# Attention and feed-forward on one core: batch 0's queries and group 0's tokens in two halves, in a newly ordered program

## The chip, the cores and the metric

The kernel runs on one core of a Trainium2 chip. The time is the device time of one execution in microseconds (us); the median of the runs counts. A profile is one more execution, recorded by the hardware profiler.

The engines are named as in the profile: PE is the matmul engine (PEld its weight loads), ACT applies functions such as exp and relu, DVE does elementwise work, POOL is used here for small copies and to issue software DMA, and SP issues hardware DMA. Each engine works through its own instructions in the order in which the program gives them.

## What is computed

```python
scores = scale * q @ k.T                    # 8 batches, 8 heads, 576 positions, 64 wide
bias   = bias_table[bucket(|i - j|)]        # constant from distance 128 on
attn   = softmax(scores + bias)
x      = (attn @ v)  as (4608 tokens, 512)
y      = relu(x @ w_in) ** 2 @ w_out        # 512 -> 2048 -> 512
```

Inputs and weights come in fp16 tiles after loading; the output is fp32. 4608 tokens are 8 batches of 576.

## The kernel before, in words

**An order made by a planner.** The kernel does not emit instructions as its loops run. Every step (one operation on one engine, with its inputs, its buffers, an estimated length and a due time) is handed to `P.add`. `P.schedule` then walks simulated engine clocks and picks, for each engine, the step that can start first; among those, the one with the smallest due time. It fixes each engine's order and which slot of a buffer ring a step uses. On the chip there is no choice left: an engine that reaches an instruction whose input is not there stands still, with everything behind it. Due times come from formulas (`nominal(p)`, `G0 + GP * g`) and are overridden by a long table, `DUES`, of step numbers and times.

**Attention.** Heads are taken in pairs; pair p belongs to batch p // 4. q and k of batches 0 and 1 are loaded as 96 rows of six positions, turned by PE (L718, twelve 96x96 transposes into an f bank), and copied to `qt` and `kt` by ACT (L680) or DVE (L682). The last 64 of the 576 positions need block-diagonal copies `qz` (L745, on DVE or POOL). Later batches are turned by SP's DMA (L701). Scores have keys on partitions: for a key tile of 128, two heads at once in two row tiles, two matmuls 512 wide (L763) into one of two set banks `st`; ACT takes exp of 1024 columns into `pt` (L776). Last queries (L789, exp L799) and last keys (L814, exp L824) have steps of their own and use set banks too. DVE multiplies by the exponential of the bias near the diagonal (L857): per pair four pieces of 512, 1536, 640 and 192 columns. Where the bias is constant, nothing is multiplied. Then PE makes the values: for each query tile nine matmuls (L893, L900), three query tiles in one step and two in another; DVE divides (L917, L922) into `x`. `pt` has three slots.

**Turning x.** For batches 0 and 1, `x_turn` turns x on PE (L960, four 128x128 for a query tile) and ACT or DVE copies it to `xt` (L680, L682).

**Feed-forward.** Tokens are in nine groups of 512. Layer 1 of a group has 16 steps, one per 128 hidden columns: four matmuls 512 wide (L1315) into one of three f banks, relu on ACT (L1344), square on DVE (L1354) into `g`. It needs all of the group's `xt` and the quarter of `w_in` that holds the columns. Layer 2 (L1084) works with sums of weights (L1014) and of activations (L1039); groups 7 and 8 do part of layer 1 with seven products in place of eight (L1239), which are fed in among the rest.

**Loads.** `loader` (L327) issues them. POOL's software queue has eight lanes and carries q, k and v of batches 0 and 1, the four quarters of `w_in`, four of `w_out` (512 KB each), and the rows of later q and k. SP and ACT issue the first q and k, the tables, and later v. In POOL's order these issues stand among its qz copies.

Of the kernel before, what the change touches and what calls it, by code (L numbers as in the profile page):

```python
# [43 lines left out]
UNITS = {7: 1, 8: 2}  # L44

# [19 lines left out]
0:118000 10:143030 32:114040 40:-9780 51:205280 56:-2470 58:-21460 60:-36430 62:-2100 64:-42740 66:-3570  # L65
70:-12220 72:-22540 74:-4430 76:-1710 80:-25480 84:-30350 88:-3160 90:-27100 94:-10280 98:-12060 102:-10140
120:5110 122:3790 124:10370 126:15880 128:17190 130:347580 132:-52240 134:-14320 136:-8260 138:-11000 140:-8690
142:-36670 144:-30540 146:-36280 148:-3170 150:-2780 152:-2780 154:-2290 156:-2220 158:-2580 160:-2620 168:-1450
170:-29000 172:-2120 174:5970 176:2720 200:17220 204:10300 206:2310 210:2020 220:10760 222:10420 226:9730
228:17470 238:412520 244:14860 256:9990 266:59150 282:8490 304:235630 312:-44250 326:288120 340:211140  # L70
383:449450 436:233270 560:-10510 562:7970 570:63210 586:-18300 588:3090 590:7540 594:8390 614:9280 618:9490
620:9600 622:9600 624:9600 644:9910 648:10090 650:8530 657:130160 660:15000 674:27510 676:78210 703:84310
730:389740 735:120980 743:21470 745:-6240 747:10350 760:424020 771:160200 774:117470 802:255000 813:21690
824:65160 892:84330 896:150530 906:116620 907:140670 914:201640 961:53470 979:52250 998:16050 1008:-16370
1051:35570 1076:6550 1096:-26430 1120:214110 1179:37190 1211:39430 1216:389710 1221:131080 1222:203470
1229:68730 1255:140120 1256:112580 1257:187030 1313:200990 1343:211010 1344:216260 1347:299680 1354:193070
1373:113930 1376:86680 1378:116480 1392:2880 1405:123690 1410:124790 1437:128150 1442:124910 1444:3730
1469:126520 1474:123310 1497:272360 1506:47770 1531:134590 1533:159790 1546:203540 1560:530 1564:117960
1586:145220 1587:144260 1618:167550 1626:54840 1676:5070 1685:70350 1690:162240 1706:278460 1709:19830
1710:292470 1742:312270 1744:290020 1759:206510 1766:233170 1780:224870 1804:197130 1807:-22280 1839:-14530  # L80
1850:3140 1895:196650 1907:22680 1923:302060 1931:294800 1935:98210 1952:321510 1957:298250 1960:319370
1979:377200 2031:5800 2044:235210 2047:324240 2052:207380 2058:222320 2116:53050 2198:-1850 2220:2260
2223:212770 2293:433240
# [159 lines left out]
def kernel(  # L243
# [78 lines left out]
    def loader(eng_name, eng, out_, in_, packets, deps=(), bufs=(), due=0.0, after=0.0, turn=-1e9):  # L322

        lane = [Buf(r_lane)] if eng_name == "POOL" else []
        issue = P.add(
            {eng_name: (775.0 if packets[0] >= 512 else 665.0) if eng_name == "POOL" else 500.0},
            lambda: io(eng.dma_start(out=out_(), in_=in_())),  # L327
            deps,
            list(bufs) + lane,
            due,  # L330
            after,
        )
        return P.land(packets, [issue], list(bufs) + lane, spare[0]), issue
# [6 lines left out]
    def const(f):  # L340
        return lambda: f

    def load(*args, **kw):
# [8 lines left out]
            const(t[0, 0:2].rearrange("h (p j) d -> p h (j d)", j=6)), (192, (60, 60)[w]), (), [b_stg[0]], due=-5,  # L352
# [7 lines left out]
        (128, 27), due=0,  # L360
# [136 lines left out]
    def load_six(p, w):  # L497
# [8 lines left out]
                (192, 61), (), [b_stg[p]], pdue(),  # L506
# [3 lines left out]
    def load_rows(p, w):  # L510
# [8 lines left out]
                (512, 13.2), s_fix, [b_stg[p]], pdue(),  # L519
            )  # L520
            for e in range(2)
# [5 lines left out]
                (128, 13.2), s_fix, [b_stg[p]], pdue(),  # L527
# [14 lines left out]
    def load_v_head(b, h):  # L542
        l = load(
            "POOL", nc.gpsimd,
            lambda: vas[b_v[b].slot][:, :, h, 0:64],
            const(v[b, h, 0:512, :].rearrange("(t p) d -> p t d", p=128)),
            (512, 13.2), v_fix[min(b, 1)], [b_v[b]], pdue(),
        )
        l_v.setdefault((b, h // 2), []).append(l)

    def load_v_tail(b):
        for e in range(2):
# [4 lines left out]
                (256, 13.2), v_fix[min(b, 1)], [b_v[b]], pdue(),  # L557
# [4 lines left out]
    def load_v(b):  # L562
        for tt in range(4):
# [4 lines left out]
                (1024, 13.2), v_fix[min(b, 1)], [b_v[b]], pdue(),  # L568
# [7 lines left out]
    def load_v_fp32(b):  # L576
# [9 lines left out]
        for tt in range(5):  # L586
            fb = Buf(r_f)
            if tt < 4:
# [5 lines left out]
                        (1024, 18.0), 690.0,  # L594
                    )
                ]
            else:
# [5 lines left out]
                        (256, 18.0), 450.0,  # L603
# [67 lines left out]
    xt_ready, x_last = {}, {}  # L671
# [17 lines left out]

    def pair(p):  # L690
# [5 lines left out]
        for w, dst in ((0, qts), (1, kts)):  # L696
            if b >= DT_QK:
# [9 lines left out]
                evac.append(P.land((640, 23.0), [o], [qb, b_stg[p]], SPARE[1]))  # L707
# [31 lines left out]
        for w, src, dst in ((0, qts, qzs), (1, kts, kzs)):  # L739
            for e in range(2):  # L740
# [6 lines left out]
                spread.append(one_of({"DVE": 205.0, "POOL": 320.0} if b < DT_QK else {"POOL": 320.0}, sp, [evac[w]] + z_fix[min(p, 1)], [qb], T - 1000))  # L747
        pb = Buf(r_pt)
        exps = {}

        def p5(t):
            return t[:, 0:PW].rearrange("p (j e s) -> p j e s", j=4, e=2)
# [91 lines left out]
        def view(o0, dims):  # L844
            t = pts[pb.slot]
            full = t[:, o0 : o0 + 1]
            return bass.AP(tensor=full.tensor, offset=full.offset, ap=[full.ap[0]] + [list(d) for d in dims])

        def tab(w0, n, rep):
            full = tb_sb[:, 2 * hp : 2 * hp + 2, w0 : w0 + n]  # L850
            return bass.AP(
                tensor=full.tensor, offset=full.offset,
                ap=[full.ap[0]] + ([[0, rep]] if rep > 1 else []) + [list(x) for x in full.ap[1:]],
            )

        def tt(a, t):
            io(nc.vector.tensor_tensor(out=a, in0=a, in1=t, op=MULT))  # L857

# [3 lines left out]
                lambda: tt(view(0, [[S, 2], [1, 256]]), tab(128, 256, 1)),  # L862
# [4 lines left out]
                lambda: tt(view(2 * S, [[2 * S + 128, 2], [S, 2], [1, 384]]), tab(0, 384, 2)),  # L867
# [4 lines left out]
                lambda: tt(view(6 * S + 256, [[S, 2], [1, 320]]), tab(0, 320, 1)),  # L872
# [8 lines left out]
        xb = x_bufs[p] = Buf(r_x)  # L881
        norms = []
        for part, qt0, nq in ((0, 0, 3), (1, 3, 2)):
            bank = Buf(r_pv)

            def pv(qt0=qt0, nq=nq, bank=bank):
                ps = pv_ps[bank.slot][:, 0 : nq * 130].rearrange("p (t e d) -> p t e d", t=nq, e=2)
                pt, pm = pts[pb.slot], p4s[pb.slot]
                va, vm = vas[b_v[b].slot], v4s[b_v[b].slot]
                for i in range(nq):  # L890
                    c = (qt0 + i) * 128
                    io(
                        nc.tensor.matmul(  # L893
                            ps[:, i, :, :], pm[:, c : c + 128], vm[:, hp, :, 0:65], start=True, stop=False
                        )
                    )
                    for e in range(2):
                        for jt in range(4):
                            io(
                                nc.tensor.matmul(  # L900
                                    ps[:, i, e, :],
                                    pt[:, (2 * jt + e) * S + c : (2 * jt + e) * S + c + 128],
                                    va[:, jt, 2 * hp + e, 0:65],
                                    start=False,
                                    stop=(jt == 3 and e == 1),
                                )
                            )

            o = P.add(
                {"PE": nq * 300.0}, pv,  # L910
                bands + list(exps.values()) + l_v[b, hp] + first, [bank, pb, b_v[b]], T + 1, after, "f",
            )
            rb = Buf(r_r)

            def recip(nq=nq, bank=bank, rb=rb):
                ps = pv_ps[bank.slot][:, 0 : nq * 130].rearrange("p (t e d) -> p t e d", t=nq, e=2)
                io(nc.vector.reciprocal(out=rs[rb.slot][:, 0:nq], in_=ps[:, :, :, 64:65]))  # L917

            def norm(nq=nq, bank=bank, rb=rb, qt0=qt0):
                ps = pv_ps[bank.slot][:, 0 : nq * 130].rearrange("p (t e d) -> p t e d", t=nq, e=2)  # L920
                io(
                    nc.vector.tensor_tensor(  # L922
                        out=xs[xb.slot][:, qt0 : qt0 + nq, :].rearrange("p t (e d) -> p t e d", e=2),
                        in0=ps[:, :, :, 0:64],
                        in1=rs[rb.slot][:, 0:nq].to_broadcast([128, nq, 2, 64]),
                        op=MULT,
                    )
                )

            o = P.add({"DVE": 190.0}, recip, [o], [bank, rb], T - 2000)  # L930
            o = P.add({"DVE": dve(nq * 128)}, norm, [o], [bank, rb, xb], T - 2000)
            norms.append(o)
# [488 lines left out]
```

## Time and profile before

| | us |
|---|---|
| runs, median (lowest to highest) | 372.38 (371.84 to 373.97) |
| the profiled execution | 371.38 |
| span of its profile | 369.6 |
| PE busy | 355.2 (96%) |
| DVE busy | 274.9 (74%) |
| ACT busy | 261.8 (71%) |
| POOL busy | 183.6 (50%) |
| first exp of attention (L776) | 9.66 |
| first layer-1 matmul (L1315) | 41.35 |
| first relu (L1344) | 42.42 |

The span runs from the first to the last recorded instruction; what lies around it is 1.8 us. "Busy" counts modelled ends, so that a PE full of back-to-back matmuls reads as 100%. In the profile's lines, `out<-in` gives the program's names of tiles, `xN` a count, and the bracket the engine's idle time before the piece and what ended it. In the page's slices a digit is the busy share of a slice of 9.24 us, in tenths.

### The profile page before, as it was taken

The page shows a single profiled execution, that of the slowest core. Times are in us where ns is not written, and L with a number is a line of the kernel's source. Part 1 is how long each engine was busy: PE and PEld are TensorE (multiplying, and loading weights), DVE is VectorE, ACT ScalarE, POOL GpSimd, SP SyncE. Part 2 cuts the span into 40 slices and gives each one's busy share as a digit, 9 for nine tenths or more (in the row PEclk, how much of TensorE's full clock was granted, in tenths as well). Part 3 has the DMA queues.
Part 4 walks back from the last instruction along what each step waited for, and adds up shares of the span by engine and source line. Part 5 has one row for each costly group of instructions (what it writes and reads, how often), then busy time and mean ns, then how long its engine had stood idle before and what let it go on. Part 6 is the DMA issues. An engine that isn't in the chain of part 4 may idle for free.

```text
span 369.6 us, 10056 instructions
## 1 busy us (share of the span) xinstructions
PE 355.2 (96%) x3966; PEld 247.2 (67%) x3966; DVE 274.9 (74%) x626; ACT 261.8 (71%) x380; POOL 183.6 (50%) x332
## 2 busy tenths in 40 slices
PE   3887999999999999999999999999999999999996
PEld 3564655756768565877766765466777877767785
DVE  4998799958884588756695666886888569586773
ACT  4998899786686789797788777977677335546600
POOL 8986249999999898777786671011000000000000
PEclk9999899999999999999999999999999999999999
DMA  9999999999999999999999994134122130020032
GB/s 160 158 167 189 197 146 150 176 156 118 191 182 164 167 170 167 130 169 161 149 178 107 158 139 105 35 66 94 48 66 53 20 106 2 28 87 28 3 114 87
DMA packets 162293, 44.26 MB, mean 120 GB/s; under 512 B 145734, under 2 KB 162246, under 8 KB 162246
## 3 DMA queue, kind: packets, MB, share of 16 engines
q0 software_dynamic: 74208, 14.53, 51.1%
q1 hardware_dynamic: 87696, 28.80, 41.4%
q8 instruction: 31, 0.51, 0.6%
q10 hardware_dynamic: 342, 0.30, 0.3%
q14 instruction: 16, 0.13, 0.1%
HBM read 36.88 MB, written 9.44 MB: 125 GB/s over the span
## 4 chain that ended last, share of the span: by engine, by line
PE 80%; DMA 7%; POOL 5%; DVE 5%; issue 1%; ACT 1%; SPq 0%; POOLq 0%
PE f L1315 28%; PE f L1084 27%; PE pv L900 8%; PE st L763 7%; DMA ks<-in_k_dram 3%; PE pv L893 2%; DMA w_in_sb<-in_moe_w_in_dram 2%; PE st L814 2%; POOL ks L327 2%; PE st L789 1%; PE st L1239 1%; DVE pt L857 1%; DMA vm<-in_v_dram 1%; POOL qs L327 1%; POOL va L327 1%; DVE s L1039 1%
## 5 line engine op out<-in xcount | busy, mean ns | idle before, releaser
L776 ACT ACTIVATE pt<-st 128x1024 f16<-128x1024 f32 x128 | 124.4, 1026 | 23.1 <-PE st L763 22.8
L1315 PE MATMUL f<-xt,w_in_sb 128*128 128x512 f16 (+4 forms) x656 | 130.8, 338 | 0.1
L1344 ACT ACTIVATE rt<-f 128x512 f16<-128x512 f32 x132 | 77.9, 606 | 39.2 <-PE f L1315 35.7
L1315 PEld LDWEIGHTS <-w_in_sb 128*128 128x128 f16 x656 | 57.6, 98 | 45.8 <-issue 9.8
L1354 DVE TENSOR_TENSOR g<-rt 128x512 f16<-128x512 f16 x132 | 57.2, 440 | 33.1 <-ACT rt L1344 32.3
L857 DVE TENSOR_TENSOR pt<-pt,tb_sb 128x512 f16<-128x512 f16 (+2 forms) x96 | 60.4, 639 | 10.7 <-ACT pt L776 10.1
L1084 PEld LDWEIGHTS <-g 128*128 128x128 f16 x576 | 54.7, 98 | 12.5 <-issue 4.2
L327 POOL DMA_DIRECT2D ks<-in_k_dram x79 | 55.8, 725 | 9.4 <-DMA w_in_sb<-in_moe_w_in_dram 2.7
L327 POOL DMA_DIRECT2D qs<-in_q_dram x79 | 55.6, 714 | 6.5 <-DMA w_out_sb<-in_moe_w_out_dram 2.9
L900 PE MATMUL pv<-va,pt 128*128 128x65 f16 x1280 | 55.8, 194 | 0.2 <-DVE pt L857 0.2
L900 PEld LDWEIGHTS <-pt 128*128 128x128 f16 x1280 | 51.1, 98 | 3.9 <-issue 0.9
L1084 PEld LDWEIGHTS <-s 128*128 128x128 f16 x432 | 40.9, 98 | 9.2 <-issue 3.4
L1112 DVE SCALAR_TENSOR_TENSOR y<-f,y 128x512 f32<-128x512 f32 (+1 forms) x47 | 31.3, 666 | 14.9 <-PE f L1084 14.5
L763 PE MATMUL st<-qt,kt 64*128 64x512 f16 x256 | 40.7, 389 | 1.5 <-ACT pt L776 0.9
L893 PE MATMUL pv<-vm,pm 128*128 128x130 f16 x160 | 35.6, 222 | 0.8 <-DVE x L922 0.7
L1084 PE MATMUL f<-wt,g 128*128 128x256 f16 x288 | 36.2, 273 | 0.0
L1084 PE MATMUL f<-w_out_sb,s 128*128 128x256 f16 x288 | 36.1, 273 | 0.0
L1084 PE MATMUL f<-w_out_sb,g 128*128 128x256 f16 x272 | 33.8, 273 | 0.1
L745 POOL COPY qz<-qt 64x64 f16<-64x64 f16 x50 | 17.2, 345 | 33.2 <-DMA qt<-qs 23.6
L922 DVE TENSOR_TENSOR x<-pv,r 128x384 f16<-128x384 f32 (+1 forms) x64 | 31.2, 487 | 1.4 <-DVE r L917 0.2
L1039 DVE TENSOR_TENSOR s<-g,s 128x1024 f16<-128x1024 f16 x36 | 26.2, 734 | 0.1
L917 DVE RECIPROCAL r<-pv 128x6 f32<-128x6 f32 (+1 forms) x64 | 11.8, 184 | 15.2 <-PE pv L900 15.0
(92 smaller groups left out, 348.9 us busy)
## 6 DMA issues: line engine op xcount, KB each, us to landing
out_dram<-y SPq DMA_DIRECT2D x34, 256.0 KB, 2.4
f<-in_v_dram SPq DMA_DIRECT2D x24, 256.0 KB, 4.1
qs<-in_q_dram POOLq DMA_DIRECT2D x48, 64.0 KB, 4.5
ks<-in_k_dram POOLq DMA_DIRECT2D x48, 64.0 KB, 4.5
w_in_sb<-in_moe_w_in_dram POOLq DMA_DIRECT2D x4, 512.0 KB, 9.7
w_out_sb<-in_moe_w_out_dram POOLq DMA_DIRECT2D x4, 512.0 KB, 15.3
ks<-in_k_dram POOLq DMA_DIRECT2D x7, 144.0 KB, 5.5
qs<-in_q_dram POOLq DMA_DIRECT2D x7, 144.0 KB, 5.4
```

The costliest lines, as they stand in the source:

```text
L327: lambda: io(eng.dma_start(out=out_(), in_=in_())),
L763: nc.tensor.matmul(sets_ps[st.slot][:, e, :], kt[rw, ts(jt, 128)], qt[rw, 0:512], start=True, stop=True,)
L776: nc.scalar.activation(out=p5(pts[pb.slot])[:, jt, :, 0:512], in_=sets_ps[st.slot], func=EXPF, scale=SCALE)
L857: io(nc.vector.tensor_tensor(out=a, in0=a, in1=t, op=MULT))
L893: nc.tensor.matmul(ps[:, i, :, :], pm[:, c : c + 128], vm[:, hp, :, 0:65], start=True, stop=False)
L900: nc.tensor.matmul(ps[:, i, e, :], pt[:, (2 * jt + e) * S + c : (2 * jt + e) * S + c + 128], va[:, jt, 2 * hp + e, 0:65], start=False, sto ...
L922: nc.vector.tensor_tensor(out=xs[xb.slot][:, qt0 : qt0 + nq, :].rearrange("p t (e d) -> p t e d", e=2), in0=ps[:, :, :, 0:64], in1=rs[rb.s ...
L1084: nc.tensor.matmul(home[bf.slot][:, ts(s_, HALF)], left(c, s_), right(c), start=(c == 0 and (s_ == 0 or apart) and (own or i not in before ...
L1112: nc.vector.scalar_tensor_tensor(out=dst, in0=ps, scalar=OSC, in1=ys[y[plus].slot][:, cs], op0=MULT, op1=mybir.AluOpType.add,)
L1315: nc.tensor.matmul(g_ps[bank.slot][:, a:z], w_in_sb[:, kk, ts(nt, 128)], xt_sb[:, kk, c : c + z - a], start=(kk == 0), stop=(kk == 3),)
L1344: io(nc.scalar.activation(out=rts[rb.slot], in_=g_ps[bank.slot], func=RELUF))
L1354: nc.vector.tensor_tensor(out=gs[gb1.slot][:, nt, :], in0=rts[rb.slot], in1=rts[rb.slot], op=MULT)
```

## The change

Batch 0's pairs are handled in two halves of their queries: half 0 takes queries 0 to 255 (two query tiles), half 1 the other 320. The first halves of all four pairs come first (`HSTEP` sets their due times), then the second halves. Two key tiles of a half share one set bank, so an exp still has 1024 columns; last keys split into 256 and 320 columns; last keys and last queries of batch 0 move from the set banks to the f banks. The bias is multiplied in three pieces in half 0 and four in half 1. Values come as two query tiles, then three. `x_turn` of batch 0 turns its first two tiles after the first halves.

Layer 1 of group 0 (`by_halves`) takes 256 tokens at a time: eight steps for each half, and a step makes two hidden tiles of 128 columns in one f bank with eight matmuls 256 wide. Its relu has 512 columns as before; the square writes two strips of 256. The first half needs only the first 256 tokens of `xt` (`xt_half[0]`).

`DUES` is replaced as a whole, and some estimated lengths of loads change, which only the planner reads. With both, the order of the whole program is new. On POOL, qz copies number 111 in place of 101; on DVE, 17 in place of 27. Three copies of the bias table move from DVE to ACT. The other kinds of work keep their number of instructions but for a few.

```diff
+HALVES, HSTEP, HL1 = 1, 1650.0, (20000.0, 34000.0)
 DUES = """
-0:118000 10:143030 32:114040 40:-9780 ...
+8:-10082 18:14645 30:300187 31:89669 ...
 """
...
+    def half_of_pair(p, part, turned):
+        hp = p % 4
+        qb, evac, spread = turned
+        T = LEAD + HSTEP * (4 * part + hp)
+        q0 = 256 * part
+        nk = 256 if part == 0 else 320
+        def scores(jt):
+            st = Buf(r_set)
+            def score():
+                for j in range(2):
+                    for e in range(2):
+                        rw = ds(64 * e, 64)
+                        io(nc.tensor.matmul(
+                            sets_ps[st.slot][:, e, ts(j, 256)], kt[rw, ts(jt + j, 128)], qt[rw, ds(q0, 256)],
+                            start=True, stop=True,
+                        ))
...
+            exps[jt] = P.add({"ACT": act(1024)}, ex, [o], [st, pb], T)
+        def last_keys():
+            st = Buf(r_g)
...
+        scores(0)
+        last_keys()
+        scores(2)
+        if part:
+            last_queries()
...
+        return values(p, part, 2 * part, 2 + part, pb, bands + list(exps.values()), T, 0.0)
...
-            deps = [n_[0 if qt < 3 else 1] for n_ in norms]
+            deps = [n_[0 if qt < (2 if b < HALVES else 3) else 1] for n_ in norms]
...
+                if b < HALVES:
+                    xt_half.setdefault(qt // 2, []).append(e)
...
+    def by_halves(g):
+        gb1 = g_bufs[g]
+        for h in range(2):
+            for u in range(8):
+                bank, rb = Buf(r_g), Buf(r_rt)
+                due = HL1[h] + 1000.0 * u
+                def f1(u=u, h=h, bank=bank):
+                    for j in range(2):
+                        for kk in range(4):
+                            io(nc.tensor.matmul(
+                                g_ps[bank.slot][:, ts(j, HALF)], w_in_sb[:, kk, ts(2 * u + j, 128)],
+                                xt_sb[:, kk, ts(h, HALF)], start=(kk == 0), stop=(kk == 3),
+                            ))
+                o = P.add({"PE": 8 * mm(HALF)}, f1, xt_half[h] + [l_win[u // 2]], [bank, gb1], due, 0.0, "f")
...
+            if g < HALVES:
+                by_halves(g)
+            for nt in [] if g < HALVES else [nt for nt in range(16) if nt % 8 >= 2 * units]:
...
         norms = [pair(4 * b + hp) for hp in range(4)]
+        if b < HALVES:
+            norms = list(zip(*([half_of_pair(4 * b + hp, part, norms[hp]) for hp in range(4)] for part in range(2))))
```

## The prediction

> **What bounds the kernel now.** I read the page's 40 slices first, then windows of five microseconds over the start, the timeline of the two thinnest windows, PE's waits, and the groups by form for durations.
>
> ```profile
> PE   3887999999999999999999999999999999999996
> DVE  4998799958884588756695666886888569586773
> ACT  4998899786686789797788777977677335546600
> ```
>
> PE is full from the fifth slice (about 37 us) to the last but one. Only the start and the tail hold idle PE time; whatever shortens the rest must take work out of PE, and this change takes none. Windows (columns: window, length, busy time of PE, PEld, DVE, ACT, POOL, PE clock, DMA share, GB/s):
>
> ```profile
> 5.00:10.00 5.00, 4.36 (x67) 3.14 (x68) 2.98 (x11) 3.50 (x7) 4.86 (x7) 1.00 1.82 172
> 15.00:20.00 5.00, 3.71 (x74) 2.20 (x74) 4.85 (x14) 4.88 (x8) 4.51 (x7) 1.00 1.46 172
> 20.00:25.00 5.00, 4.04 (x90) 2.90 (x84) 4.79 (x13) 4.84 (x6) 3.95 (x6) 1.00 1.65 177
> 25.00:30.00 5.00, 4.25 (x83) 3.04 (x81) 4.84 (x14) 4.89 (x8) 4.67 (x9) 1.00 1.42 159
> 30.00:35.00 5.00, 3.30 (x57) 2.29 (x53) 3.99 (x13) 4.28 (x7) 2.58 (x13) 1.00 1.22 188
> 35.00:40.00 5.00, 4.59 (x60) 3.62 (x61) 3.78 (x12) 3.24 (x5) 2.87 (x5) 0.66 1.23 198
> 40.00:45.00 5.00, 5.00 (x47) 2.46 (x44) 4.10 (x13) 4.68 (x8) 1.09 (x3) 1.00 1.22 199
> 32.60:36.00 3.40, 2.02 (x40) 1.44 (x40) 2.51 (x8) 1.95 (x5) 2.48 (x13) 1.00 1.25 204
> 36.00:39.40 3.40, 3.40 (x40) 2.65 (x37) 2.26 (x7) 2.54 (x4) 1.27 (x4) 0.50 1.23 198
> ```
>
> From 15 to 30 us ACT and DVE are full (4.8 to 4.9 of 5) and PE waits on them: all it has is attention of batch 0. From 30 to 40 nobody is full: ACT falls to 3.24. Then PE runs at half clock for 3.4 us. At 41.35 layer 1 starts and PE is full. The timeline shows why 30 to 40 is thin (start, duration, engine and line, idle before with releaser):
>
> ```profile
> 35.41 0.45 PE L718 MATMUL f<-id_sb,ks 96*64 96x96 f16 x12 [1.27 <-DMA ks<-in_k_dram]
> 35.90 0.65 ACT L680 ACTIVATE kt<-f 128x576 f16<-128x576 f16 x1 [1.45 <-PE f L718]
> 39.35 1.23 ACT L824 ACTIVATE pm<-st 128x576 f16<-128x576 f32 x2 [0.72 <-PE st L814]
> 41.35 1.03 PE L1315 MATMUL f<-xt,w_in_sb 128*128 128x512 f16 x4
> ```
>
> PE stands before a transpose of keys whose DMA has not landed, and ACT stands behind PE. The chain of waits names the transfer: issued at 26.07, it took 9.29.
>
> ```profile
> 26.07 9.29 DMA ks<-in_k_dram
> ```
>
> A busy PE overstates, since ends are modelled. So I counted slots from start to start: 216 ns for a 512-wide matmul, 109 for a 256-wide, 29 for a 65-wide one. PE's work is 332.4 us, and 145 switches between row-tiled scores and whole-array matmuls take 0.1 each, 14.5. The rest of the span is loss: 5.5 before the first matmul; in five-microsecond steps from 5 us on 2.5, 0.5, 1.45, 1.5, 1.2, 2.5 and 1.9; later 2.7 in all; 3.1 after the last matmul. Up to 40 us that is 5.5 + 11.55 = **17.05 us**, the only store a change of order can draw on.
>
> **The change part by part.** *Layer 1 of group 0 in halves.* 64 matmuls of 216 ns become 128 of 109: 13.95 - 13.82 = +0.13 us on PE. The 109 is a slot between 256-wide matmuls whose weights also change each time:
>
> ```profile
> L1084 PE MATMUL f<-wt,g 128*128 128x256 f16 x288 | 36.2, 273 | 0.0
> ```
>
> and from the chain, with start and length:
>
> ```profile
> 81.68 1.73 PE f L1315 x8
> 164.84 1.75 PE f L1084 x16
> ```
>
> (1.73/8 = 216 ns, 1.75/16 = 109). Here a rule speaks against the change: the Trainium skill, TensorE: Matmul & The Clock Gate, Back-to-back issue gap, gives for a stream of weight load and matmul about 81 ns at width 128 and 131 at 512. Interpolated, 256 wide would take some 98, and halving would cost 128 x 98 - 64 x 131 = +4.1 us, turning the forecast into a loss. The trace has 216 and 109, so I keep +0.13. Weight loads double (64 more of 98 ns) but fit under 109. The relu stays 128x512 (606 ns). The square writes two strips of 256: nearest row 440 ns (128x512), at most the 500 of a 640 band; x16 that is 0 to +1 us on DVE, behind PE's matmuls once layer 1 runs.
>
> *Batch 0 in halves.* On PE the scores keep their columns: 32 of 512 become 64 of 256, +0.05. Program order has 151 switches in place of 145: +0.6. **PE work: about +0.8 us in all**, paid for certain. On ACT the last keys' exp splits 576 into 256 and 320. By the rows of 512 (604), 576 (657) and 1024 (1026) an exp takes about 172 ns + 0.832 per column, so 385 + 438 against 651: +0.17 x 4 = +0.7; three table copies (0.6 each) move from DVE to ACT, +1.8. On DVE the bands of a pair go from 465 + 952 + 500 + 258 to seven pieces, by the same rows +0.5 x 4; the table copies (0.69 x 3) and ten qz copies (about 0.25) leave: DVE is not longer. POOL gets those ten copies, 0.33 each, **ahead of loads in its queue** (rival C). Splits below a row's size carry +-0.1 each; over the 20 pieces I take 0, keep -0.5 to +1.
>
> *What is moved.* Layer 1 can start when two token tiles of batch 0 are turned. ACT's order up to the first relu, at saturated spacing (0.915 for 1024, 0.545 for 576, 0.49 for 512): before 18 x 0.915 + 13 x 0.545 + 9 x 0.49 = 28.0; it started at 9.66 and came to its first relu at 42.42, so it waited 4.8. After: 16 x 0.915 + 9.8 for the rest = 24.4, none of it exps of pair 4. At the start q is cast first and the copies to q and k of pair 0 follow directly; from the cast and copy rows the first exp comes at about 8.5, 1.1 earlier. ACT then gets to the relu at about 33 if it never waits.
>
> *PE's ledger after.* First matmul: 5.5 as before. 5 to 10: 2.5 becomes 1.4 (first exp earlier). 10 to 30: ACT-bound in both, 4.65 kept. By then PE has done 18.8 us of work and switches, and 18.8 + 11.55 gives the first layer-1 matmul at about 30.3, where before it came at 41.35 after 24.7 of work. From 30 to 42 PE has 256-wide layer-1 groups to stand between pairs. What I find late next: the second group needs w_in's second quarter (about 35.1), keys of pair 5 (about 32.9), and POOL's copies for pair 5 (about 0.9 us of waiting). A walk by hand gives 0.9 to 1.3 there in place of 4.4; a walk has no jitter, and the queues of before showed 9.29 us for one small load, so I add 0.7 to 1.2: **2.0**. Sum: 5.5 + 1.4 + 4.65 + 2.0 = 13.5.
>
> *The clock.* Of the 4.4 lost, 1.7 is the half clock from 36.0 to 39.4. The trace shows it after a window in which PE was busy 2.02 of 3.40, with no gap over 1.27. The same page of the Trainium skill, HAM oscillation, warns of PE-idle gaps over about 3.4 us; by that, nothing here should slow it. By the rule the after has no dip (12.5 to 12.8); by the trace one window thinner than 60% costs 1.7 again. PE stays thin near 30 us, so I count half, which is within the 0.7 to 1.2 added.
>
> *The rest.* Due times are new everywhere, but PE was full from 45 to 345 us and its work is the same; between 100 and 200 us DVE (72%) and ACT (80%) have room. Pairs 8 to 12 stand 7 to 10 us of PE work later, so POOL's and SP's loads for them have more margin than before. Mid-span: 0, -0.5 to +1. Tail: the last weight-sum product stands 24 x 109 = 2.6 us ahead of its user where its chain of copies takes about 2.3; before it was 7.9. So 0 to +0.7; I take 0.
>
> Sum: 17.05 - 13.5 - 0.8 = **2.75 us gain**. The profiled execution took 371.38 (span 369.6 and 1.8 around), 1.0 below the median 372.38. I apply the difference to the median: 372.38 - 2.75 = **369.6**. A measurement can tell about 0.5%, 1.86 us: faster is below 370.5, slower above 374.2.
>
> **The rivals.** *A, the walk holds exactly* and the dip goes too (0.14): loss 12.5 to 12.8, gain 3.4 to 3.8, about 368.8; for it, layer 1 has its data by 29; against it, no engine of before ran without stalls.
> *B, the gain is not there* (0.25): ACT collects waits again. Its loads ride the same software queue; loss then 15.5 to 16.5, gain -0.2 to +0.8, about 372.0. Or the gain is taken back: PE earlier by 3 meets loads that the queue delivers at the same time (the chain at 117.44 runs through a 3.99 us load of v), or the tail takes 0.7. For it: 19.2 us, the longest landing of a weight quarter.
> *C, slower* (0.10): POOL's queue. In the changed order w_in's second quarter and pair 5's keys stand behind qz copies that wait for copies on ACT and DVE; the last of them, for pair 4's keys, lets go at about 23 to 25. The quarter is then issued at about 25.2, and PE wants it at 35.1. The four weight quarters of before landed in 6.7 to 19.2, median 9.7: 34.9 at the median. In-order PE stands still behind it, 1 us per us: the gain is gone with a landing after 37.9, and slower than the bound after 39.7, 14.5 after issue. At 41 the time is about 375.5.
>
> **How the numbers follow.** The forecast 0.51, A 0.14, B 0.25, C 0.10. Faster by over 0.5%: nearly all of A, the forecast but for its top, a little of B: 0.66. Same: 0.25. Slower: C and a piece of B's tail, 0.09. Range: A with its bounds at 367.0; B whole and the lower part of C at 373.4.
>
> **What would show it.** Right: first exp near 8.5, first layer-1 matmul near 30, no PE gap over 1 us between 30 and 42, clock 1.0 throughout, PE's loss by 42 us near 13.5. Wrong: a PE wait on w_in or ks of over 2 us in 30 to 42 (C); ACT under 4.3 of 5 between 15 and 30 (B); half clock again in 30 to 42; a gap in PE after 45 us that before doesn't have; a last sevens product waited for at 345.

## The result and the profile after

The changed kernel took 367.75 us in the median of four runs (366.33 to 368.46), the kernel before 373.01 of four: ratio 0.9856, 95% interval 0.981 to 0.990. A second set of runs (`again` below, 6 and 19 runs) gave 0.9903, 0.988 to 0.993, which is 3.6 us. The profiled executions had spans of 366.7 against 369.6 us, 2.9 apart, and in the second pair of traces 365.5 against 369.0, 3.5 apart. The two intervals meet only between 0.988 and 0.990. The larger set and the traces agree on a gain of 3 to 3.6 us, and that is what is explained here; that the 5.3 us of the first medians come from the spread of few runs is likely, not shown.

The page of the changed kernel (slices of 9.17 us):

```profile
PE   3988999999999999999999999999999999999996
...
ACT  5999998479975789678986778967778444725620
```

PE's first digits are 3, 9, 8, 8 where they were 3, 8, 8, 7. Its windows:

```profile
15.00:20.00 5.00, 3.84 (x87) 2.44 (x82) 4.54 (x19) 5.00 (x9) 4.24 (x9) 1.00 1.28 142
20.00:25.00 5.00, 5.00 (x94) 3.39 (x94) 4.35 (x15) 5.00 (x9) 4.16 (x7) 1.00 1.49 160
25.00:30.00 5.00, 4.49 (x82) 3.23 (x80) 4.92 (x16) 5.00 (x10) 4.96 (x8) 1.00 1.66 160
30.00:35.00 5.00, 4.16 (x95) 3.63 (x94) 3.58 (x15) 4.55 (x9) 3.45 (x13) 1.00 1.43 190
35.00:40.00 5.00, 4.85 (x73) 3.43 (x69) 4.18 (x12) 4.63 (x8) 3.54 (x9) 1.00 1.25 207
```

ACT (fourth of the busy times) is full from 15 to 30, and 30 to 40 is no longer thin: PE has 4.16 and 4.85 of 5 at full clock, where it had 3.30, and 4.59 at a clock of 0.66. The timeline:

```profile
7.87 0.69 PE L930 MATMUL f<-id_sb,qs 96*64 96x96 f16 x12 [0.80 <-DMA qs<-in_q_dram]
...
9.15 1.02 ACT L822 ACTIVATE pt<-st 128x1024 f16<-128x1024 f32 x1
...
19.77 0.28 PE L835 MATMUL f<-qt,qz 128*128 128x256 f16 x1 [0.75 <-POOL qz L957]
...
30.72 1.04 PE L1442 MATMUL f<-xt,w_in_sb 128*128 128x256 f16 x8
...
34.24 0.45 PE L930 MATMUL f<-id_sb,ks 96*64 96x96 f16 x12 [0.84 <-DMA ks<-in_k_dram]
...
36.31 1.04 PE L1442 MATMUL f<-xt,w_in_sb 128*128 128x256 f16 x8
```

The first exp is at 9.15, layer 1 (L1442) starts at 30.72, its second group at 36.31. Pair 5's keys still hold PE, for 0.84 us.

PE's loss is the time to its last matmul, less its work and 0.1 us for each switch between row-tiled scores, 96x96 transposes and whole-array matmuls (the switches to and from scores measure 92 to 97 ns here). Counted alike in every trace, to about 0.3 us:

| trace | loss by 40 us | later | first layer-1 matmul |
|---|---|---|---|
| before | 16.55 | 3.0 | 41.35 |
| before, second trace | 15.05 | 3.9 | 39.96 |
| after | 13.2 | 2.7 | 30.72 |
| after, second trace | 11.6 | 3.0 | 30.4 |

In the first pair that is 3.4 + 0.3 less loss; less 0.8 of added work and switches (332.6 against 332.4 us, 151 against 145) it makes 2.9, the difference of the spans.

### The profile page after: what moved, and what is told of

Read it like the earlier page. It is cut to its first block, busy times and chain, and to the rows that moved or that the text cites. A ratio compares the mean times of both kernels' runs of the same rounds, so it can differ in the third digit from the quotient of the medians.

```text
span 366.7 us, 10230 instructions
## 1 busy us (share of the span) xinstructions
PE 354.2 (97%) x4062; PEld 253.5 (69%) x4062; DVE 272.2 (74%) x622; ACT 263.0 (72%) x390; POOL 187.1 (51%) x342
## 4 chain that ended last, share of the span: by engine, by line
PE 83%; DVE 6%; DMA 4%; POOL 2%; issue 2%; ACT 2%; POOLq 0%
PE f L1218 27%; PE f L1489 27%; PE pv L746 9%; PE st L974 7%; PE pv L739 2%; PE f L1442 2%; DMA w_in_sb<-in_moe_w_in_dram 2%; DMA qs<-in_q_dram 2%; PE st L1025 2%; PE st L1000 2%; DVE s L1173 1%; PE st L1373 1%; DVE pt L713 1%; ACT rt L1518 1%; POOL va L346 1%
## 5 line engine op out<-in xcount | busy, mean ns | idle before, releaser
L987 ACT ACTIVATE pt<-st 128x1024 f16<-128x1024 f32 x112 | 108.9, 1030 | 26.8 <-PE st L974 26.1
L1489 PE MATMUL f<-xt,w_in_sb 128*128 128x512 f16 (+4 forms) x592 | 111.8, 333 | 0.0
L1518 ACT ACTIVATE rt<-f 128x512 f16<-128x512 f32 x116 | 67.9, 609 | 25.8 <-PE f L1489 23.4
L1489 PEld LDWEIGHTS <-w_in_sb 128*128 128x128 f16 x592 | 51.7, 98 | 43.4 <-issue 9.3
L713 DVE TENSOR_TENSOR pt<-pt,tb_sb 128x512 f16<-128x512 f16 (+3 forms) x108 | 60.5, 578 | 13.4 <-ACT pt L987 12.5
L1528 DVE TENSOR_TENSOR g<-rt 128x512 f16<-128x512 f16 x116 | 51.4, 449 | 22.7 <-ACT rt L1518 21.1
L746 PE MATMUL pv<-va,pt 128*128 128x65 f16 x1280 | 54.8, 193 | 0.2 <-DVE pt L713 0.2
L746 PEld LDWEIGHTS <-pt 128*128 128x128 f16 x1280 | 50.2, 97 | 2.5 <-issue 0.6
L957 POOL COPY qz<-qt 64x64 f16<-64x64 f16 x54 | 18.4, 342 | 32.9 <-DMA qt<-qs 17.5
L974 PE MATMUL st<-qt,kt 64*128 64x512 f16 x224 | 33.9, 381 | 0.0
L760 DVE RECIPROCAL r<-pv 128x6 f32<-128x6 f32 (+1 forms) x64 | 11.8, 184 | 17.0 <-PE pv L746 16.5
```

What stands on the lines that cost most here:

```text
L746: nc.tensor.matmul(ps[:, i, e, :], pt[:, (2 * jt + e) * S + c : (2 * jt + e) * S + c + 128], va[:, jt, 2 * hp + e, 0:65], start=False, sto ...
L974: nc.tensor.matmul(sets_ps[st.slot][:, e, :], kt[rw, ts(jt, 128)], qt[rw, 0:512], start=True, stop=True,)
L987: nc.scalar.activation(out=p5(pts[pb.slot])[:, jt, :, 0:512], in_=sets_ps[st.slot], func=EXPF, scale=SCALE)
L1489: nc.tensor.matmul(g_ps[bank.slot][:, a:z], w_in_sb[:, kk, ts(nt, 128)], xt_sb[:, kk, c : c + z - a], start=(kk == 0), stop=(kk == 3),)
L1518: io(nc.scalar.activation(out=rts[rb.slot], in_=g_ps[bank.slot], func=RELUF))
L1528: nc.vector.tensor_tensor(out=gs[gb1.slot][:, nt, :], in0=rts[rb.slot], in1=rts[rb.slot], op=MULT)
```

## The experiments

All ratios are to the kernel before, run on the same chip in the same session. Line numbers of variants can differ by a few.

**again: the changed kernel, a second trace.**

> The changed kernel once more, for a second trace and a tighter ratio. Theory: the trace accounts for 2.9 us (3.4 less loss on PE by 40 us, 0.3 less later, 0.8 more work and switches), so the ratio to the kernel before is near 0.992, and the first layer-1 matmul comes at 30 to 31 us as in the first trace. Rival: the medians of the first runs (0.986, 5.3 us) are the truth, and the kernel before has a loss in most executions that its one trace does not show, of about 2 us; then its ratio stays near 0.986.

Ratio 0.9903 (0.9879 to 0.9926). Nearer to what the traces account for than to the first medians. Its windows show the mechanism without disturbance (no late keys):

```profile
25.00:30.00 5.00, 4.60 (x90) 3.44 (x88) 4.92 (x16) 5.00 (x9) 4.96 (x9) 1.00 1.61 161
30.00:35.00 5.00, 5.00 (x112) 4.14 (x109) 4.28 (x16) 5.00 (x9) 4.57 (x16) 1.00 1.45 193
35.00:40.00 5.00, 5.00 (x69) 3.98 (x67) 4.61 (x14) 5.00 (x8) 2.56 (x7) 1.00 1.24 202
```

From 30 on both PE and ACT are full: attention fills ACT, layer 1 fills what that leaves of PE.

**before_again: the kernel before, a second trace.**

> The kernel before once more, one look, for a second trace. Theory (its half-clock piece of 3.4 us follows from a thin window behind a late load of keys): the piece, 1.7 us of loss, comes again near 36 us, or it is missing where pair 5's keys land earlier than 35.4; PE's loss by 40 us stays between 14.8 and 17.5. Rival (the clock piece is chance): the same gaps, no piece; or a piece at another place, and a span over 371.

The half-clock piece is missing here, as the theory allowed: pair 5's keys did not hold PE (no such wait in the timeline), and 30 to 35 was less thin:

```profile
30.00:35.00 5.00, 4.21 (x79) 3.14 (x78) 4.71 (x16) 4.92 (x8) 3.54 (x14) 1.00 1.23 194
35.00:40.00 5.00, 4.79 (x86) 3.56 (x87) 4.63 (x15) 4.77 (x8) 2.87 (x5) 1.00 1.21 193
```

Its loss by 40 us is 1.5 smaller than in the first trace, though its first exp came later (10.5 against 9.66); 0.9 more is lost afterwards, so the span fell by only 0.6. Against this trace, which has no piece, the change gains 3.5 us (`again`) or 2.3 (its first trace): the piece is not where most of the gain comes from.

**all_turned: the early start undone.** The planner then orders the program anew: up to 30 us on PE and to 35 us on POOL the order is that of `again`, loads included; behind that it differs on every engine, and the due times were not fitted to it.

```diff
-                o = P.add({"PE": 8 * mm(HALF)}, f1, xt_half[h] + [l_win[u // 2]], [bank, gb1], due, 0.0, "f")
+                o = P.add({"PE": 8 * mm(HALF)}, f1, xt_half[0] + xt_half[1] + xt_half[2] + [l_win[u // 2]], [bank, gb1], due, 0.0, "f")
```

> The changed kernel, but each layer-1 step of group 0 must wait until all five token tiles of batch 0 are turned; the first halves lose their early start, and all else up to there keeps its order. Theory (PE had nothing to do between 30 and 40 us, and the early steps fill it): four steps of 8 x 109 ns, 3.5 us of PE work, stood before 41 us in the changed kernel; they now come after 40 us, and the time is 2 to 3.5 us longer than the changed kernel's. Rival (the new order of loads and copies, or the missing half-clock piece of 1.7 us, brings the gain, layer 1 only follows): within 0.7 us of the changed kernel.

Ratio 1.0006 (0.9986 to 1.0026): 3.8 us longer than `again`, the whole gain and a little over the expected 3.5. Its timeline:

```profile
33.57 0.45 PE L930 MATMUL f<-id_sb,ks 96*64 96x96 f16 x12 [0.93 <-DMA ks<-in_k_dram]
...
37.81 0.38 PE L1000 MATMUL st<-qz,kt 128*128 128x128 f16 x4 [0.61 <-ACT pm L1035]
...
40.14 1.91 PE L1442 MATMUL f<-xt,w_in_sb 128*128 128x256 f16 x16
```

Layer 1 starts at 40.14; loss by 40 us is 14.0 (11.6 in `again`), later 4.9 (3.0). The new order of loads, the halves of attention and the 256-wide steps are all still there, full clock too (from 14.0 us on), and bring nothing. The rival falls. The theory holds for the 2.4 us by 40; the 1.9 us behind may as well come from due times that no longer fit.

**whole_attention: layer 1 in halves, batch 0 whole.**

```diff
-        if b < HALVES:
+        if b < HATT:                  # HATT = 0, in pair, at its call and in x_turn
             return qb, evac, spread
```

> Layer 1 of group 0 in halves, as in the changed kernel, but batch 0's pairs whole, as before (their due times from the kernel before; all other due times from the changed one; its own order follows). Theory (it is the early x that counts: with whole pairs the first 256 tokens are turned only after all exps of batch 0, so layer 1 comes at about 39 to 42 us): within 1 us of the kernel before, first layer-1 matmul at 38 or later. Rival (halving layer 1 alone gives PE work in small pieces, and that is the gain): 2 us or more shorter than before.

First layer-1 matmul at 44.87, and 1.0205 (1.0169 to 1.0242). That layer 1 does not start early was expected; the 7.6 us over the kernel before were not. Two sets of due times were mixed, so its order fits neither; PE had 18.7 us of loss by 40. So its time does not tell what halving layer 1 alone is worth.

**plain_whole and plain_halves: the same pair without fitted due times.**

```diff
-DUES = """
-8:-10082 18:14645 30:300187 31:89669 ...
-"""
+DUES = ""
-HALVES, HSTEP, HL1 = 1, 1650.0, (20000.0, 34000.0)
+HALVES, HSTEP, HL1 = 0, 1650.0, (20000.0, 34000.0)      # plain_whole only
```

> The changed file with its halves switched off (batch 0 and group 0 whole) and no due times from the list, only those of the formulas. It is the base for plain_halves; program order puts its first layer-1 matmul behind 21.6 us of PE work and 35 switches. Theory and rival alike: slower than the kernel before, by 1 to 8 us, since nothing was fitted.

> The changed file with its halves on and no due times from the list. Program order puts its first layer-1 matmul behind 18.8 us of PE work and 37 switches, as early as in the changed kernel. Theory (the early half of layer 1 is the gain, whatever the order of the rest): 2 to 4 us shorter than plain_whole. Rival (the gain is only had with the fitted due times; whole_attention, half fitted, was 7.6 us slower than before): within 1 us of plain_whole, or longer.

1.0107 (1.0075 to 1.0139) and 1.014 (1.009 to 1.019): no gain, so on the time the rival is right. Nor did layer 1 start as early as in the changed kernel: at 37.0 with halves, at 42.1 without. The two traces show where time went in one execution each, the slowest of its runs. Windows of plain_whole, then of plain_halves:

```profile
30.00:60.00 30.00, 27.14 (x327) 15.84 (x327) 24.89 (x67) 24.73 (x37) 17.24 (x37) 0.94 1.26 181
60.00:80.00 20.00, 17.41 (x195) 10.84 (x194) 16.88 (x35) 13.90 (x21) 19.67 (x32) 1.00 1.56 151
150.00:180.00 30.00, 29.62 (x362) 21.57 (x360) 21.36 (x50) 24.43 (x36) 25.05 (x45) 1.00 1.43 158
```

```profile
30.00:60.00 30.00, 29.72 (x454) 23.39 (x451) 27.58 (x80) 28.48 (x46) 18.54 (x39) 1.00 1.26 183
60.00:80.00 20.00, 17.41 (x195) 11.95 (x194) 15.90 (x32) 11.54 (x15) 19.08 (x33) 0.83 1.57 137
150.00:180.00 30.00, 27.27 (x321) 19.96 (x320) 19.97 (x47) 23.16 (x34) 26.73 (x51) 1.00 1.53 156
```

With halves, PE's loss by 60 us is 14.6 where plain_whole has 18.7. Of these 4.1 us, 1.7 are a half-clock piece of plain_whole (42.25 to 45.66) that by the mean clock nine of its eleven runs do not have; about 2.4 are left as the gain in the start. From 60 to 80 plain_halves loses 2.7 more than plain_whole (a wait of 1.71 on a band at 65.05, and half clock from 65.5 to 72.3), from 150 to 180 2.7 more: the gain is given back. That it is the fitted order of the rest that keeps it in the changed kernel is likely, not shown. And no run has whole pairs with due times fitted as newly as the changed kernel's, so what the new fit alone is worth stays open.

**w_in_late: a late second quarter of w_in.**

```diff
+    before(l_win[1].deps[0], l_win[2].deps[0])     # in the finished order, on POOL
```

> The changed kernel with the second quarter of w_in issued just ahead of the third instead of four issues earlier on POOL, about 3.5 us later (25.6 becomes 29). In the changed kernel it landed 2.8 us ahead of the first matmul that needs it (33.5 against 36.3). Theory (rival C's price: PE stands behind the quarter once that margin is gone, 1 us per us): landing at 36.5 to 38, and 0.2 to 2 us on the time. Other view (the load is only one of several in a queue bound by bytes; keys and weights that it makes room for come earlier, so nothing is lost): within 0.3 us of the changed kernel; or the landing is over 40 and the gain is gone, 3 us.

1.0111 (1.0077 to 1.0145), **7.7 us** over `again` by the two ratios, and 6.2 by the spans (the traced run is its fastest). Both views were too mild. A line of the chain, and one of the timeline:

```profile
28.04 11.76 DMA w_in_sb<-in_moe_w_in_dram
```

```profile
39.84 1.89 PE L1447 MATMUL f<-xt,w_in_sb 128*128 128x256 f16 x8 [4.75 <-DMA w_in_sb<-in_moe_w_in_dram]
```

The quarter, issued at 28.04 with the third right behind it, took 11.8 us to land and not 7.85, and the group behind it took 1.89 us where 1.04 stands in the changed kernel's timeline. The clock halves during the wait of 4.75 us, at 37.68, and stays so for 6.83 us; the 4.7 us of it that lie behind the wait cost about 2.3 more:

```profile
34.26:37.68 3.42, 0.83 (x26) 0.71 (x22) 2.06 (x7) 1.92 (x3) 1.85 (x6) 1.00 1.23 202
37.68:41.09 3.41, 1.25 (x6) 0.89 (x7) 0.00 (x0) 0.00 (x0) 0.45 (x1) 0.50 1.20 194
41.09:44.50 3.41, 3.41 (x21) 2.60 (x19) 0.88 (x3) 1.69 (x3) 0.00 (x0) 0.50 1.23 197
```

**scores_first: pair 0's scores ahead of pair 1's q.**

```diff
+    after(tags["turn", 1, 0], tags["scores", 0, 0, 2])
+    after(tags["copy", 1, 0], tags["exp", 0, 0, 0])
+    for e in range(2):
+        after(tags["spread", 1, 0, e], l_qk[4, 1][0].deps[0])
```

> The changed kernel, with three groups of instructions moved: pair 1's q transposes go behind pair 0's first scores on PE, their copy on ACT behind the first exp, and the two qz copies of it behind the load of pair 4's keys. In the changed kernel PE waited 0.80 us for pair 1's q at 7.87 with pair 0's scores behind it, and the first exp came at 9.15 where 8.5 was forecast. Theory (ACT is full from its first exp to 34 us and sets the pace of PE up to there): first exp at about 8.45, and the time 0.4 to 0.7 us shorter. Rival (POOL's queue sets the pace: PE waited 0.75 us on a qz copy at 19.77): no more than 0.2 us.

0.9892 (0.9873 to 0.9911) against 0.9903: in the expected direction, inside the interval. The first exp came at 8.83 and not 8.45: the first k landed later in this execution (its cast on ACT began at 5.85, in `again` at 5.34). `again` had its first exp at 8.82 without the edit, so the traces do not show the step that was to bring the time.

**tables_dve, tables_dve2: two table copies from ACT to DVE.** tables_dve put the copies behind a matmul that refills their bank, so part of its bias table was another part's; 0.9944 says nothing on the edit. It had half clock from 15.7 to 25.9. Its edit, and that of tables_dve2, which leaves them at their places:

```diff
+    for o in sorted([o for o in tabs_done if o.eng == "ACT"], key=order.index)[0:2]:
+        o.eng = "DVE"
+        before(o, on_dve[0])        # tables_dve only: DVE's own first copy
```

> The changed kernel with two of the four table copies that it has on ACT (0.5 us of ACT each) on DVE, which stood idle 1.29 us before its own. Theory (ACT is full from its first exp on, 15 to 40 us at 5.00 of 5, and sets PE's pace): ACT is 1.0 us less behind, PE loses 0.6 to 1.0 less by 40 us, and the time is 0.4 to 1.0 shorter. Rival (DVE, or POOL's copies, set the pace as much as ACT): within 0.3 us or longer.

> The changed kernel with the first two of ACT's four table copies made by DVE, at their own places in the order (tables_dve had put them behind a matmul that refills the bank, so a part of its table was wrong and its time says nothing on this). DVE is idle 1.29 us ahead of its own table copies. Theory (ACT, full from 15 to 40 us, sets PE's pace): 0.4 to 1.0 us shorter than the changed kernel, no half-clock piece. Rival (DVE is as tight: 4.57 and 4.92 of 5 in two windows, and gets 1.3 us more): within 0.3 us or longer; if a 3.4 us window of PE falls under 0.6 busy, a half-clock piece as in tables_dve, and longer by 1 to 2.

tables_dve2: 0.9899 (0.9866 to 0.9933), the changed kernel's time. One us less of ACT work, and a first exp at 8.50, move nothing, so ACT is not alone in setting the pace from 10 to 30; the theory falls in this form. Loss from 10 to 30 was 3.65 us, in `again` 3.7. Which of DVE, POOL's copies and PE's own order takes over was not separated.

**three and best: edits together.** three joined scores_first, the table copies of tables_dve (the same part of its table replaced) and the exchange of two loads on POOL; best is that without the table copies.

```diff
+    i, j = order.index(l_qk[7, 1][0].deps[0]), order.index(l_qk[5, 1][0].deps[0])
+    order[i], order[j] = order[j], order[i]        # in both, with the lines of scores_first
```

> The changed kernel with three edits: pair 0's scores ahead of pair 1's q (as in scores_first), two table copies on DVE (as in tables_dve), and on POOL the load of pair 5's keys in the place of pair 7's, and the other way round. The last takes away a wait of 0.84 us that PE had for these keys at 34.24 in one trace of two. Theory: the parts add up, 1 to 2 us shorter than the changed kernel, ratio to before near 0.986. Rival (something else becomes the bound after one of them): no more than 0.5 us.

> The changed kernel with pair 0's scores ahead of pair 1's q (as in scores_first) and, on POOL, the load of pair 5's keys in the place of pair 7's and the other way round. Theory: the start gives 0.3 to 0.5 us as scores_first did, and pair 5's keys, late by 0.84 us in one trace of the changed kernel and 0.93 in all_turned, never hold PE; ratio to the kernel before 0.986 to 0.989. Rival (pair 7's keys, four issues later, become the wait; or the first loads' own spread, 0.5 us from run to run, covers it all): ratio as the changed kernel's 0.990 or above.

three: 0.9965, with half clock from 16.6 to 23.5; its table copies spoil the reading. best: 0.9895 (0.9867 to 0.9924). PE has no wait for keys in its trace and its first exp is at 8.29, yet its loss by 40 us is 12.5: between the two traces of the changed kernel. No version was found that is clearly shorter than the changed kernel.

## Why the prediction was right, point by point

- **Where the gain comes from: right, and shown** as far as the order goes that was fitted to it: without the early start of layer 1 the changed kernel has no gain (all_turned, 1.0006). Layer 1 was forecast at 30.3 and came at 30.72 and 30.4; before it came at 41.35.
- **The store of loss: 0.5 too high.** "5.5 before the first matmul" and "2.5" from 5 to 10 us overlap by half a microsecond. On one count before has 16.55 by 40 us and the forecast for after is 13.0; measured 13.2 and 11.6.
- **"2.5 becomes 1.4": failed.** The loss from 5 to 10 us was 3.1 in both traces, larger than before; the 0.5 us by which the first transposes came sooner (5.03 against 5.52) makes up for part of it. Two things were wrong. The order puts pair 1's q transposes ahead of pair 0's scores, and PE stood 0.80 us for that load; the first exp came at 9.15, not 8.5. And the 2.5 were not mainly a wait that an earlier exp ends: before had no gap of PE over 0.15 us from 5.52 to 12 us, but its matmuls ran at about half speed; its first full clock is on record at 12.1. The twelve transposes that took 0.45 us at 35.41 took more here:

```profile
8.38 0.69 PE L718 MATMUL f<-id_sb,ks 96*64 96x96 f16 x12
```

In all_turned, whose order is the same up to 30 us, the load came in time and the first exp as forecast, and by the same count about 2.6 us were lost all the same:

```profile
8.35 1.02 ACT L822 ACTIVATE pt<-st 128x1024 f16<-128x1024 f32 x1 [0.17 <-PE st L812]
```

- **"4.65 kept" from 10 to 30: 0.8 to 0.9 too high.** 3.9 and 3.7 were lost: PE is 5.00 of 5 from 20 to 25, where before had 4.04.
- **"2.0" from 30 to 42:** 1.4 and 0.2. Pair 5's keys cost 0.84 in one trace and nothing in the other; the jitter that was added is real, but it is not there each time. The errors of these three terms largely cancel in the first trace (13.2 against 13.0), which is luck; in the second 1.4 us are left over (11.6).
- **+0.8 of PE work: as measured.** 332.6 against 332.4 and six more switches. (The 145 and 151 switches take in those to and from the 96x96 transposes; changes to and from row-tiled scores alone are 134 and 136.) A 256-wide group of eight takes 0.87 us in the chain, so 109 ns each; the 98 worked out from the skill's page does not hold here, nor does its 131 for 512 wide: eight such took 1.73 us in the chain of before, 216 each.
- **The median.** 369.6 was forecast, a gain of 2.75; 3.6 by the larger set of runs, 2.9 and 3.5 by the two pairs of traces.
- **Rival B, the gain given back:** not in the changed kernel (later loss 2.7 to 3.0, before 3.0 to 3.9), but it is what happened in plain_halves, without fitted due times. It deserved its weight; what keeps it away is probably in the list of due times, which I had only costed by its margins.
- **Rival C, a late quarter of w_in: right in its place, mis-sized in its price.** The quarter landed at 33.48 (issued 25.63, 7.85 us) against a need at 36.31: 2.8 us of margin. Past the margin it is not 1 us per us: 4.75 of waiting cost 6 to 8, about 2.3 of it by the clock that halved during the wait.
- **The clock: counted half, none came.** Neither trace of the changed kernel has a piece at half clock between its first full clock, at 12.4 and 12.5 us, and its end. See below.

## What to carry to other kernels

Where one engine is full of one kind of work and the other waits on it, look for the smallest part of the next stage whose inputs can be had early, and arrange the first stage so that they come early; a second stage that is split alone still waits for the whole of the first. Count the gain in the place where it arises and again at the end: in a fixed order it can be given back tens of us later. And price a wait on PE with the clock that follows from it.

## What was not expected of the hardware

The granted clock follows a fixed grid of 3.41 us. All its pieces at half clock in these traces, up to the last matmuls, last 3.41, 6.83 or 10.24 us, and the grid lies differently in each execution (the first full clock came between 12.1 and 17.7 us). A fall to half clock goes with how little of the window before it PE was busy, by the profile's own count. Windows on the grid, from the kernel before, tables_dve, whole_attention (two) and all_turned:

```profile
32.60:36.01 3.41, 2.03 (x40) 1.44 (x40) 2.52 (x8) 1.96 (x5) 2.49 (x13) 1.00 1.26 205
```

```profile
12.27:15.68 3.41, 1.97 (x62) 1.76 (x61) 2.40 (x4) 2.10 (x3) 2.39 (x4) 1.00 1.31 117
```

```profile
18.81:22.23 3.42, 1.37 (x10) 0.68 (x9) 3.41 (x6) 3.42 (x6) 3.13 (x7) 1.00 0.90 68
35.88:39.29 3.41, 2.12 (x49) 1.77 (x47) 2.29 (x8) 2.69 (x6) 2.23 (x7) 1.00 1.30 196
```

```profile
31.03:34.45 3.42, 2.35 (x49) 1.59 (x47) 3.09 (x10) 2.52 (x6) 2.26 (x11) 1.00 1.46 175
```

After 2.03, 1.97 and 1.37 of 3.41 (60, 58 and 40%) the next window ran at half clock; after 2.12 and 2.35 (62 and 69%) it did not. The same holds for every full-clock window on the grid of all fourteen traces, up to 10 us before the end: all seven falls came after a window of 59.5% or less (the thinnest 24%, in w_in_late), and no other window was under 62%. In these traces the line lies between 59.5 and 62%; no run set the share on purpose, so this is a rule that fits, not a cause that is shown. It does not tell when full clock returns: in `three` PE was busy for all of 16.63 to 20.04, at half clock, and the next window was at half clock again.

No gap of PE in the first of these windows was over 1.27 us, so the rule of the Trainium skill that the prediction weighed (TensorE: Matmul & The Clock Gate, HAM oscillation: gaps over about 3.4 us) is too mild here: a window thinner than about 0.6 is enough. Whether a thin stretch fills one window or is shared by two is then a matter of where the grid falls. In the trace of before a window of 3.41 us is under 0.6 only if it starts between 31.7 and 32.9 us, so by estimate from that trace about one position of the grid in three meets it. The second trace of before does not show this chance, since there the keys landed in time and its thinnest window on the grid between 30 and 37 us was at 81%:

```profile
30.26:33.67 3.41, 2.75 (x52) 1.96 (x48) 3.21 (x13) 3.33 (x6) 2.43 (x10) 1.00 1.22 192
```

That late keys and the place of the grid together make up the spread of its runs (369 to 375) is likely, not shown.
